# Linear attention beside a top-8 expert layer on one core: order of the first loads, of four VectorE steps in the opening tiles, and of one late scaling

## The chip, the core and the metric

The kernel runs on one core of a Trainium2 chip. A core has five engines that each run their own instruction list in order: TensorE (PE; its weight loads are shown as a lane of their own, PEld), VectorE (DVE), ScalarE (ACT), GpSimd (POOL) and SyncE (SP). An engine waits for another, or for a transfer, only through semaphores; whatever stands behind a waiting instruction on the same engine waits too. Transfers are issued from the lists of SP, ACT and POOL and are carried by 16 DMA engines. The metric is the device time of one execution in microseconds (us), lower is better.

## The reference, cut to what matters

For an input `x` of 2048 tokens by 640 features the result is the sum of `x`, a linear attention of the normalised `x`, and `x` plus the output of an expert layer for its 8 best tokens:

```python
xn = _layernorm(x)                                   # mean, variance, scale per token
q, k, v = split(xn @ wqkv)                           # 32 heads of 20
phi = lambda t: jnp.where(t > 0, t + 1, jnp.exp(t)) + 1e-6
kv  = einsum("bhsd,bhse->bhde", phi(k), v)
z   = einsum("bhsd->bhd", phi(k))
o   = einsum(phi(q), kv) / (einsum(phi(q), z) + 1e-6)
attention = o.reshape(B, S, D) @ wo
r = x @ w_r;  idx = argsort(-r)[:8]                  # 8 tokens for the expert layer
y = (silu(x[idx] @ w_gate) * (x[idx] @ w_up)) @ w_down * sigmoid(r[idx])
return x + attention + (x with y added to its 8 rows)
```

## The kernel before, in words

The order of all work is written out by hand: each engine runs what the program issues to it, in the order of the program. Tokens are cut into 16 tiles of 128 (`t`), features into 5 chunks of 128 (`kc`, `m`).

**Loads.** Lines 109 to 118 issue the first transfers. On SP's list stand half of x tile 0, x tile 1, two chunks of `wk`, x tile 2, `wq` in two pieces by chunk rows (chunks 0 to 2, then 3 and 4; line 117), and x tiles 4 to 7 in one transfer. On ACT's list stand the other half of x tile 0, three chunks of `wk`, and x tile 3 (line 115). The row of the transposes further down (line 198) is issued from SP as well.

**Stage 1, tiles 0 to 15.** For each tile:

- `ln_half` (line 165) takes the statistics of one half of a tile on VectorE; `ln_aggr` (lines 169 to 181) joins them, and GpSimd takes the square root as a power (line 178). For tiles 0 to 3 VectorE does the small steps around it (lines 173, 177, and the reciprocal in line 191); from tile 4 on GpSimd does all four small steps (lines 173, 178, 180, 181).
- `ln_norm` (line 193) writes the normalised tile `xn` on VectorE. Tiles 0 to 2 are transposed on TensorE (line 202) and copied out by ACT or VectorE (line 208). From tile 3 on a DMA transpose from SP writes `xnT` (line 198).
- `k_mm` (line 240) and `q_mm` (line 252) multiply on TensorE. `q_mm` runs over output chunks `m` outside and over `kc` inside, so the first output chunk needs all five row chunks of `wq`, but only columns 0 to 127.
- `phi_act` (lines 215, 218) takes exp and relu on ACT; `phi_vec` (line 227, a SCALAR_TENSOR_TENSOR with two tiles in SBUF as inputs) joins them on VectorE. Its result is `pk` for k, and `pqT` for q.
- `ga_mm` (line 263) multiplies `xn` by `pk` of one tile and sums over tiles in PSUM.

The opening is written out for tiles 0 to 2 (lines 416 to 434). From there the loop of line 437 runs for t = 2 to 15: TensorE gets k of tile t, `ga_mm` of tile t-1, q of tile t; VectorE gets the statistics of tile t+3, the normalisation of tile t+2, `phi_vec` for q of tile t-1, `phi_vec` for k of tile t.

TensorE's list in the opening is: k of tile 0, k of tile 1, q of tile 0, the transposes of tile 2, `ga_mm(0)`, q of tile 1, k of tile 2, `ga_mm(1)`, q of tile 2, k of tile 3, `ga_mm(2)`, and so on.

**Stage 2 and 3.** The sums over all tiles are finished, the 8 tokens are selected, denominators and the expert layer are computed, and `M` is built in five chunks (`m_chunk`, line 743; `m_copy`, line 754). `norm(a, b)` (line 683) scales `pqT` of the output tiles a to b-1 by the reciprocal denominators `rb` on VectorE. It is called for tiles 0 and 1 together ahead of the expert's `py` products (line 766) and of `y_sb` (line 774), and for the others behind `m_copy(3)`. The output products `out_mm` (line 795) then run tile by tile; tile 0 needs the scaled `pqT` of tile 0, tile 1 that of tile 1.

Of the kernel before, what the change touches and what calls it, by code (L numbers as in the profile page):

```python
# [8 lines left out]
P = 128  # L9
S = 2048  # L10
D = 640
# [4 lines left out]
KC = D // P  # L16
# [31 lines left out]
def kernel(  # L48
# [13 lines left out]
    nc = tc.nc  # L62
# [4 lines left out]
    x_v = A_x[0].rearrange("(t p) d -> p t d", p=P)  # L67
    out_v = out[0].rearrange("(t p) d -> p t d", p=P)
    wqkv_v = A_wqkv.rearrange("(kc p) n -> p kc n", p=P)
# [6 lines left out]
    def sb(shape, dt, name, tag=None):  # L76
        return big.tile(shape, dt, tag=tag or name, name=name)
# [4 lines left out]
    def bank(tag, name):  # L82
        return psum.tile([P, TBLK], F32, tag=tag, name=name)

    x_sb = sb([P, T, D], BF16, "x_sb")
# [3 lines left out]
    pk = sb([P, T, D], BF16, "pk")  # L89
    wk = sb([P, KC, D + 1], BF16, "wk")  # L90
    wq = sb([P, KC, D], BF16, "wq")
# [20 lines left out]
    nc.scalar.dma_start(wk[:, 0:3, 0:D], wqkv_v[:, 0:3, D : 2 * D])  # L112
    nc.sync.dma_start(wk[:, 3:KC, 0:D], wqkv_v[:, 3:KC, D : 2 * D])
    nc.sync.dma_start(x_sb[:, 2, :], x_v[:, 2, :])
    nc.scalar.dma_start(x_sb[:, 3, :], x_v[:, 3, :])
    for a, b in ((0, 3), (3, KC)):
        nc.sync.dma_start(wq[:, a:b, :], wqkv_v[:, a:b, 0:D])
    nc.sync.dma_start(x_sb[:, 4:8, :], x_v[:, 4:8, :])


# [41 lines left out]
    def ln_half(t, h):  # L162
        if h == 0:
            stat[t] = work.tile([P, 2, nc.vector.BN_STATS_DIM], F32, tag="stats", name=f"st{t}")
        nc.vector.bn_stats(out=stat[t][:, h, :], in_=x_sb[:, t, h * HW : (h + 1) * HW])  # L165

    def ln_aggr(t):
        mv = work.tile([P, 2], BF16, tag="mv", name=f"mv{t}", bufs=4)
        nc.vector.bn_aggr(out=mv[:], in_=stat[t][:])
        sc = work.tile([P, 2], F32, tag="sc", name=f"sc{t}", bufs=4)  # L170
        sq = work.tile([P, 2], BF16, tag="sq", name=f"sq{t}", bufs=4)
        scal[t] = sc, sq
        (nc.vector if t < LN_FAST else nc.gpsimd).tensor_scalar(  # L173
            out=sq[:, 0:1], in0=mv[:, 1:2], scalar1=EPS_BF16, scalar2=None, op0=ALU.add
        )
        if t < LN_FAST:
            nc.vector.tensor_copy(sc[:, 0:1], mv[:, 0:1])
        nc.gpsimd.tensor_tensor(out=sq[:, 1:2], in0=sq[:, 0:1], in1=half[:], op=ALU.pow)  # L178
        if t >= LN_FAST:
            nc.gpsimd.tensor_tensor(out=sc[:, 1:2], in0=sq[:, 1:2], in1=neg1[:], op=ALU.pow)  # L180
            nc.gpsimd.tensor_copy(sc[:, 0:1], mv[:, 0:1])  # L181

    def ln_stats(t):
        ln_half(t, 0)
        ln_half(t, 1)
        ln_aggr(t)

    def ln_norm(t):
        sc, sq = scal[t]
        if t < LN_FAST:  # L190
            nc.vector.reciprocal(sc[:, 1:2], sq[:, 1:2])
        for a, b in ((0, 2 * P), (2 * P, D)) if t == 0 else ((0, D),):
            nc.vector.tensor_scalar(  # L193
                out=xn[:, t, a:b], in0=x_sb[:, t, a:b], scalar1=sc[:, 0:1], scalar2=sc[:, 1:2],
                op0=ALU.subtract, op1=ALU.mult,
            )
        if t >= PE_TR:
            nc.sync.dma_start_transpose(xnT[:, :, t * P : (t + 1) * P], xn[:, t, :])

    def tr_tile(t, ptr, lo, hi):  # L200
        for kc in range(lo, hi):
            nc.tensor.transpose(
                ptr[:, kc * P : (kc + 1) * P], xn[:, t, kc * P : (kc + 1) * P], ident[:]
            )

    def tr_evict(t, ptr, lo, hi, copy):
        src = ptr[:, 0:D].rearrange("p (k f) -> p k f", k=KC)
        copy(xnT[:, lo:hi, t * P : (t + 1) * P], src[:, lo:hi, :])  # L208
# [3 lines left out]
    def phi_act(ps, tag, between=None):  # L212
        e = work.tile([P, D], BF16, tag="e" + tag, name="e" + tag)
        r = work.tile([P, D], BF16, tag="r" + tag, name="r" + tag)
        nc.scalar.activation(e[:], ps[:, 0:D], AF.Exp)  # L215
        if between is not None:
            between()
        nc.scalar.activation(r[:], ps[:, 0:D], AF.Relu)  # L218
        return e, r

    def phi_vec(dst, er, as3):
        e, r = er
        ea, ra = e[:], r[:]
        if as3:
            ea = ea.rearrange("p (k f) -> p k f", k=KC)
            ra = ra.rearrange("p (k f) -> p k f", k=KC)
        nc.vector.scalar_tensor_tensor(  # L227
            out=dst, in0=ea, scalar=1.0, in1=ra, op0=ALU.min, op1=ALU.add
        )
# [18 lines left out]
    def q_mm(t, tag="B"):  # L248
        ps = pair(tag, f"q{t}")
        for m in range(KC):  # L250
            for kc in range(KC):
                nc.tensor.matmul(  # L252
                    ps[:, m * P : (m + 1) * P],
                    lhsT=wq[:, kc, m * P : (m + 1) * P],
                    rhs=xnT[:, kc, t * P : (t + 1) * P],
                    start=(kc == 0 and m in (0, 4)), stop=(kc == KC - 1),
                    skip_group_check=True,
                )
        return ps

    def ga_mm(t):
        for c in range(3):
            nc.tensor.matmul(  # L263
                gaC[:, c * TBLK : (c + 1) * TBLK] if c < 2 else gaD[:],
                lhsT=xn[:, t, c * P : (c + 1) * P],
                rhs=pk[:, t, 0:TBLK],
                start=(t == 0), stop=(t == T - 1),
            )
# [129 lines left out]
    def k_phi(t, kp, pr=None):  # L398
        ker = phi_act(kp, "k")
        if t < T - 1:  # L400
            nc.scalar.copy(r_all[:, t : t + 1], kp[:, D : D + 1])
        else:
            nc.scalar.copy(rT[:], pr[0:NTB, 0:TBLK])
        return ker
# [10 lines left out]

    kp = k_mm(0, "A", transposes_1)
    ln_aggr(2)
    ln_stats(3)
    ker = k_phi(0, kp)
    kp = k_mm(1, "B")  # L420
    qp = q_mm(0, "A")
    ln_norm(2)
    phi_vec(pk[:, 0, :], ker, False)
    tr2 = bank("D1", "tr2").bitcast(BF16)
    tr_tile(2, tr2, 0, KC)
    ker = k_phi(1, kp)
    eq0 = phi_act(qp, "q", lambda: tr_evict(2, tr2, 0, KC, nc.scalar.copy))
    ln_norm(3)
    ln_stats(4)
    ga_mm(0)  # L430
    phi_vec(pk[:, 1, :], ker, False)
    qp = q_mm(1, "B")
    q_phi(0, eq0)
    qer = phi_act(qp, "q")
# [2 lines left out]
    for t in range(2, T):  # L437
# [22 lines left out]
        ker = k_phi(t, kp, pr)  # L460
# [220 lines left out]
    def norm(a, b):  # L681
        sl = pqT[:, :, a * P : b * P]
        nc.vector.tensor_tensor(out=sl, in0=sl, in1=rb[:, :, a * P : b * P], op=ALU.mult)  # L683
# [52 lines left out]
    def m_chunk(c, tag):  # L736
        pm = Acc(tag, f"M{c}")
        for a, b in halves:
            for g in range(4):
                q = 4 * c + g  # L740
                w = q * GW // KVW
                assert E0[w] <= q * GW // DH * DH and (q * GW + GW - 1) // DH * DH + DH <= E0[w] + P
                nc.tensor.matmul(  # L743
                    pm.at(a, b)[GW * g : GW * g + GW, :],
                    lhsT=kvT[:, q * GW : (q + 1) * GW],
                    rhs=wo[:, w, a:b],
                    start=True, stop=True,
                    tile_position=(0, GW * g),
                )
        return pm  # L750

    def m_copy(c, pm, copy):
        for a, b in pm.spans:
            copy(M[:, c, a:b], pm.at(a, b))
# [2 lines left out]
    m_copy(0, pm0, nc.scalar.copy)  # L757
    pm1 = m_chunk(1, "C")
    m_copy(1, pm1, nc.scalar.copy)
    norm(0, 2)  # L760

    py = pair("A", "py")
    for fc in range(FC):
        j, b = fc // 3, fc % 3
# [20 lines left out]
    m_copy(3, pm3, nc.vector.tensor_copy)  # L785
    pm4 = m_chunk(4, "A")
    m_copy(4, pm4, nc.scalar.copy)
    norm(2, 4)
    norm(4, 8)

# [33 lines left out]
    for t in range(NPRE, T):  # L824
# [6 lines left out]
        else:  # L831
            for i in range(3):
                a, b = LAST[i : i + 2]
# [39 lines left out]
```

## Time and profile before

| | |
|---|---|
| median of 3 runs | 110.91 us (109.94 to 111.06) |
| the profiled execution's own time | 109.81 us |
| its span, from first to last instruction | 108.0 us |
| busy, PE | 102.8 us (95%) |
| busy, PE weight loads | 68.4 us (63%) |
| busy, DVE | 79.9 us (74%) |
| busy, ACT | 66.4 us (61%) |
| busy, POOL | 35.4 us (33%) |
| mean granted TensorE clock | 1.0 |

Rows of the timeline read: start in us from the start of the span, duration in us, engine, line, operation, output and inputs with shapes, number of instructions; a bracket tells how long the engine was idle before it and what ended that. Instructions of an engine overlap a little: the start of the next row can lie before the end of the one ahead. A matmul's recorded duration holds its way through the array, so that the distance between starts tells the rate. Rows of the transfer table give the size and the time from issue to landing. Rows of a table of stretches give for each stretch its length, busy times, granted clock, the share of the 16 DMA engines that was busy, and the rate in GB/s.

### The profile page before, as it was taken

To read this page: it belongs to the slowest core of one execution; us is meant where nothing else is said; L and a number is where in the kernel's file an instruction comes from. 1 tells how busy PE (TensorE), PEld (TensorE's weight loads), DVE (VectorE), ACT (ScalarE), POOL (GpSimd) and SP (SyncE) were. 2 spreads that over 40 slices of the span, in tenths; PEclk is the share of its full clock that TensorE was granted. 3 is DMA by queue.
4 is the path that set the end of the run, shared out by engine and by line. 5 is a ranking of instruction groups with operands and counts; after the bars stand their busy time and mean duration, and the time that the engine had idled before them with its cause. 6 is when DMAs were issued, how large, how long until landed. Compare 5 with 4: busy or idle time off the path is not lost.

```text
span 108.0 us, 2937 instructions
## 1 busy us (share of the span) xinstructions
PE 102.8 (95%) x1132; PEld 68.4 (63%) x1146; DVE 79.9 (74%) x200; ACT 66.4 (61%) x119; POOL 35.4 (33%) x81
## 2 busy tenths in 40 slices
PE   6999999999999999999999999999999999999980
PEld 2547867776677766777677744456996555555550
DVE  3879999979999799987999886814038705938670
ACT  4358977779777797778877855469029455555000
POOL 5423096988897757681000000210003300000000
PEclk9999999999999999999999999999999999999999
DMA  2999053995597999999999991685674798999883
GB/s 67 299 377 345 13 61 61 259 99 155 90 285 154 245 331 204 370 367 187 318 352 394 389 393 53 140 294 116 193 235 150 233 304 262 276 311 393 313 289 122
DMA packets 27406, 25.64 MB, mean 237 GB/s; under 512 B 10880, under 2 KB 25472, under 8 KB 27392
## 3 DMA queue, kind: packets, MB, share of 16 engines
q1 hardware_dynamic: 25232, 23.70, 76.8%
q10 hardware_dynamic: 1984, 1.71, 4.8%
q0 software_dynamic: 176, 0.04, 0.6%
q8 instruction: 9, 0.15, 0.5%
q14 instruction: 5, 0.04, 0.2%
HBM read 17.37 MB, written 5.94 MB: 216 GB/s over the span
## 4 chain that ended last, share of the span: by engine, by line
PE 84%; DVE 9%; DMA 2%; issue 1%; POOL 1%; DVEq 0%
PE q L252 19%; PE k L240 18%; PE o L795 14%; PE gbA L533 6%; PE gaC L263 6%; PE gbC L630 4%; PE gaD L263 3%; DVE st L165 3%; DMA x_sb<-in_A_x_dram 2%; PE gu L643 2%; DVE xn L193 1%; DVE o_all L803 1%; PE pkv L708 1%; PE M L743 1%; PE zp L503 1%
## 5 line engine op out<-in xcount | busy, mean ns | idle before, releaser
L252 PEld LDWEIGHTS <-wq 128*128 128x128 bf16 x400 | 23.6, 98 | 3.6
L240 PE MATMUL k<-wk,xnT 128*128 128x129 bf16 (+1 forms) x152 | 24.5, 296 | 0.5
L252 PE MATMUL q<-xnT,wq 128*128 128x128 bf16 x400 | 25.0, 219 | 0.0
L795 PEld LDWEIGHTS <-pqT 128*128 128x128 bf16 x165 | 12.7, 98 | 9.3 <-issue 0.3
L215 ACT ACTIVATE eq<-q 128x640 bf16<-128x640 f32 x16 | 11.2, 703 | 10.2 <-PE q L252 10.1
L240 PEld LDWEIGHTS <-xnT 128*128 128x128 bf16 x160 | 12.3, 98 | 8.0 <-ACT xnT L208 0.5
L795 PE MATMUL o<-M,pqT 128*128 128x128 bf16 (+1 forms) x108 | 15.7, 298 | 0.1
L165 DVE BATCH_NORM_STATS2 st<-x_sb 128x6 f32<-128x320 bf16 x32 | 14.1, 478 | 1.0 <-DMA x_sb<-in_A_x_dram 1.0
L227 DVE SCALAR_TENSOR_TENSOR pk<-ek,rk 128x640 bf16<-128x640 bf16 x16 | 13.2, 824 | 2.2 <-ACT rk L218 1.7
L178 POOL TENSOR_TENSOR sq<-sq,half 128x1 bf16<-128x1 bf16 x16 | 12.4, 772 | 6.3 <-DVE sq L173 3.2
L227 DVE SCALAR_TENSOR_TENSOR pqT<-eq,rq 128x640 bf16<-128x640 bf16 x16 | 13.1, 818 | 0.2 <-ACT rq L218 0.2
L215 ACT ACTIVATE ek<-k 128x640 bf16<-128x640 f32 x16 | 11.2, 703 | 1.7 <-DVE r_all L441 0.3
L218 ACT ACTIVATE rq<-q 128x640 bf16<-128x640 f32 x16 | 11.2, 700 | 0.0
L218 ACT ACTIVATE rk<-k 128x640 bf16<-128x640 f32 x16 | 11.2, 698 | 0.0
L819 ACT CAST o_all<-o 128x640 bf16<-128x640 f32 x9 | 6.2, 692 | 6.1 <-PE o L795 6.1
L180 POOL TENSOR_TENSOR sc<-sq,neg 128x1 f32<-128x1 bf16 x12 | 9.0, 754 | 0.9
L683 DVE TENSOR_TENSOR pqT<-pqT,rb 128x2560 bf16<-128x2560 bf16 (+1 forms) x5 | 6.0, 1222 | 4.5 <-DMA rb<-rscr 4.4
L263 PE MATMUL gaC<-pk,xn 128*128 128x512 bf16 x31 | 9.3, 377 | 0.1
L581 POOL COPY xsT<-xnT 128x5 bf16 x8 | 1.2, 222 | 20.5 <-DVE zc L583 20.5
L193 DVE TENSOR_SCALAR xn<-x_sb,sc 128x640 bf16<-128x640 bf16 (+2 forms) x17 | 6.9, 410 | 1.0 <-POOL sc L181 0.8
L533 PE MATMUL gbA<-pk,xn 128*128 128x512 bf16 x30 | 7.2, 380 | 0.2 <-issue 0.2
L387 DVE TENSOR_TENSOR x_sb<-x_sb,xn 128x640 bf16<-128x640 bf16 x16 | 7.2, 484 | 0.0
(155 smaller groups left out, 121.7 us busy)
## 6 DMA issues: line engine op xcount, KB each, us to landing
xcp<-x_sb SPq DMA_DIRECT2D x4, 640.0 KB, 7.4
x_sb<-in_A_x_dram SPq DMA_DIRECT2D x3, 640.0 KB, 4.6
x_sb<-xcp SPq DMA_DIRECT2D x3, 640.0 KB, 8.4
out_dram<-o_all SPq DMA_DIRECT2D x11, 160.0 KB, 5.1
wg<-in_B_w_gate_dram SPq DMA_DIRECT2D x2, 768.0 KB, 6.1
wu<-in_B_w_up_dram SPq DMA_DIRECT2D x2, 768.0 KB, 6.8
rb<-rscr SPq DMA_DIRECT2D x5, 256.0 KB, 4.7
rb<-rscr SPq DMA_DIRECT2D x8, 128.0 KB, 3.4
```

Of the source, the lines that this page charges most:

```text
L165: nc.vector.bn_stats(out=stat[t][:, h, :], in_=x_sb[:, t, h * HW : (h + 1) * HW])
L178: nc.gpsimd.tensor_tensor(out=sq[:, 1:2], in0=sq[:, 0:1], in1=half[:], op=ALU.pow)
L180: nc.gpsimd.tensor_tensor(out=sc[:, 1:2], in0=sq[:, 1:2], in1=neg1[:], op=ALU.pow)
L193: nc.vector.tensor_scalar(out=xn[:, t, a:b], in0=x_sb[:, t, a:b], scalar1=sc[:, 0:1], scalar2=sc[:, 1:2], op0=ALU.subtract, op1=ALU.mult,)
L215: nc.scalar.activation(e[:], ps[:, 0:D], AF.Exp)
L218: nc.scalar.activation(r[:], ps[:, 0:D], AF.Relu)
L227: nc.vector.scalar_tensor_tensor(out=dst, in0=ea, scalar=1.0, in1=ra, op0=ALU.min, op1=ALU.add)
L240: nc.tensor.matmul(ps[:, a:b], lhsT=xnT[:, kc, t * P : (t + 1) * P], rhs=wk[:, kc, a:b], start=(kc == 0), stop=(kc == KC - 1),)
L252: nc.tensor.matmul(ps[:, m * P : (m + 1) * P], lhsT=wq[:, kc, m * P : (m + 1) * P], rhs=xnT[:, kc, t * P : (t + 1) * P], start=(kc == 0 an ...
L263: nc.tensor.matmul(gaC[:, c * TBLK : (c + 1) * TBLK] if c < 2 else gaD[:], lhsT=xn[:, t, c * P : (c + 1) * P], rhs=pk[:, t, 0:TBLK], start ...
L533: nc.tensor.matmul(gbA[:, (c - 3) * TBLK : (c - 2) * TBLK], lhsT=xn[:, t, c * P : (c + 1) * P], rhs=pk[:, t, 0:TBLK], start=(t == 0), stop ...
L795: nc.tensor.matmul(ps, lhsT=pqT[:, m, t * P : (t + 1) * P], rhs=M[:, m, a:b], start=(m == M_ORDER[0]), stop=(m == M_ORDER[-1]),)
```

## The change

Four edits:

1. x tile 3 is issued from SP behind x tile 2 and no longer from ACT; `wq` is loaded in two pieces by columns (0 to 383, then 384 to 639, all five row chunks in each) and no longer by row chunks.
2. In the opening, the statistics of tile 3 are split: the first half stays where all of it stood, the second half and the joining step move behind `phi_vec` for k of tile 0.
3. `phi_vec` for k of tile 1 (and `ga_mm(0)` in the program's text) moves ahead of the normalisation of tile 3 and of the statistics of tile 4. No order but VectorE's changes by it: the lists of TensorE, ACT and GpSimd hold the same instructions in the same order.
4. The scaling of the first two output tiles is done one tile at a time: tile 0 where both stood, tile 1 behind `m_copy(4)` in the text, which on VectorE is behind the copy of chunk 3.

VectorE's list in the opening, before: statistics of tile 3 (two halves), joining and its two small steps, reciprocal and normalisation of tile 2, `pk` of tile 0, reciprocal and normalisation of tile 3, statistics of tile 4, joining, `pk` of tile 1, `pqT` of tile 0, statistics of tile 5, joining, normalisation of tile 4, `pqT` of tile 1, `pk` of tile 2.

After: first half of the statistics of tile 3, reciprocal and normalisation of tile 2, `pk` of tile 0, second half, joining and two small steps for tile 3, `pk` of tile 1, reciprocal and normalisation of tile 3, statistics of tile 4, joining, `pqT` of tile 0, and from there as before.

```diff
-    nc.scalar.dma_start(x_sb[:, 3, :], x_v[:, 3, :])
-    for a, b in ((0, 3), (3, KC)):
-        nc.sync.dma_start(wq[:, a:b, :], wqkv_v[:, a:b, 0:D])
+    nc.sync.dma_start(x_sb[:, 3, :], x_v[:, 3, :])
+    for a, b in ((0, 3 * P), (3 * P, D)):
+        nc.sync.dma_start(wq[:, :, a:b], wqkv_v[:, :, a:b])
     nc.sync.dma_start(x_sb[:, 4:8, :], x_v[:, 4:8, :])
...
     kp = k_mm(0, "A", transposes_1)
     ln_aggr(2)
-    ln_stats(3)
+    ln_half(3, 0)
     ker = k_phi(0, kp)
     kp = k_mm(1, "B")
     qp = q_mm(0, "A")
     ln_norm(2)
     phi_vec(pk[:, 0, :], ker, False)
+    ln_half(3, 1)
+    ln_aggr(3)
     tr2 = bank("D1", "tr2").bitcast(BF16)
     tr_tile(2, tr2, 0, KC)
     ker = k_phi(1, kp)
     eq0 = phi_act(qp, "q", lambda: tr_evict(2, tr2, 0, KC, nc.scalar.copy))
+    ga_mm(0)
+    phi_vec(pk[:, 1, :], ker, False)
     ln_norm(3)
     ln_stats(4)
-    ga_mm(0)
-    phi_vec(pk[:, 1, :], ker, False)
     qp = q_mm(1, "B")
...
     m_copy(1, pm1, nc.scalar.copy)
-    norm(0, 2)
+    norm(0, 1)
...
     m_copy(4, pm4, nc.scalar.copy)
+    norm(1, 2)
     norm(2, 4)
     norm(4, 8)
```

## The prediction, made before the changed kernel was run

> **What bounds the kernel now.** I read the page's chain first, because a busy share of 95% for TensorE does not tell whether an opening edit can matter; then the timeline of the opening, engine by engine; then the transfers; last the timeline around the scaling of the output tiles.
>
> ```profile
> span 108.0 us, 2937 instructions
> PE 84%; DVE 9%; DMA 2%; issue 1%; POOL 1%; DVEq 0%
> ```
>
> The chain that ended last lies on TensorE for 84% of the span. TensorE's rows show where it last waited in the opening:
>
> ```profile
> 9.87 1.56 PE L252 MATMUL q<-xnT,wq 128*128 128x128 bf16 x25
> 11.26 0.44 PE L202 MATMUL tr<-ident,xn 128*128 128x128 bf16 x5
> 11.75 0.59 PE L263 MATMUL gaC<-pk,xn 128*128 128x512 bf16 x2
> 12.40 1.56 PE L252 MATMUL q<-xnT,wq 128*128 128x128 bf16 x25
> 17.17 1.26 PEld L240 LDWEIGHTS <-xnT 128*128 128x128 bf16 x10
> 18.61 0.59 PE L263 MATMUL gaC<-pk,xn 128*128 128x512 bf16 x2
> ```
>
> The 25 matmuls of q(0) take 11.26 - 9.87 = 1.39 us, 0.056 each, so the five transposes of tile 2 are through at 11.26 + 0.28 = 11.54. ga(0) starts only at 11.75. That wait of 0.21 us is the last one ahead of the steady loop, and all that the opening edits can win. From there TensorE goes without a gap through q(1), k(2), ga(1), q(2), k(3) (weights at 17.17) and ga(2) at 18.61. Whatever later makes TensorE wait there is lost one for one. The rows that feed it:
>
> ```profile
> 8.91 0.16 DVE L173 TENSOR_SCALAR sq<-mv 128x1 bf16<-128x1 bf16 x1
> 8.98 0.14 DVE L177 CAST sc<-mv 128x1 f32<-128x1 bf16 x1
> 9.15 0.55 POOL L178 TENSOR_TENSOR sq<-sq,half 128x1 bf16<-128x1 bf16 x1 [2.22 <-DVE sq L173]
> 10.33 0.15 DVE L191 RECIPROCAL sc<-sq 128x1 f32<-128x1 bf16 x1
> 10.52 0.45 DVE L193 TENSOR_SCALAR xn<-x_sb,sc 128x640 bf16<-128x640 bf16 x1
> 10.63 0.70 ACT L218 ACTIVATE rk<-k 128x640 bf16<-128x640 f32 x1
> 10.88 0.82 DVE L227 SCALAR_TENSOR_TENSOR pk<-ek,rk 128x640 bf16<-128x640 bf16 x1
> 11.81 0.45 DVE L193 TENSOR_SCALAR xn<-x_sb,sc 128x640 bf16<-128x640 bf16 x1
> 12.17 0.88 DVE L165 BATCH_NORM_STATS2 st<-x_sb 128x6 f32<-128x320 bf16 x2
> 13.08 0.21 DVE L169 BATCH_NORM_AGGREGATE mv<-st 128x2 bf16<-128x12 f32 x1
> 13.21 0.77 DVE L227 SCALAR_TENSOR_TENSOR pk<-ek,rk 128x640 bf16<-128x640 bf16 x1
> 13.48 0.59 POOL L173 TENSOR_SCALAR sq<-mv 128x1 bf16<-128x1 bf16 x1 [2.48 <-DVE mv L169]
> 13.90 0.82 DVE L227 SCALAR_TENSOR_TENSOR pqT<-eq,rq 128x640 bf16<-128x640 bf16 x1
> 14.16 0.98 POOL L178 TENSOR_TENSOR sq<-sq,half 128x1 bf16<-128x1 bf16 x1
> 14.63 0.88 DVE L165 BATCH_NORM_STATS2 st<-x_sb 128x6 f32<-128x320 bf16 x2
> 15.22 0.55 POOL L180 TENSOR_TENSOR sc<-sq,neg 128x1 f32<-128x1 bf16 x1
> 15.73 0.19 POOL L181 CAST sc<-mv 128x1 f32<-128x1 bf16 x1
> 15.95 0.45 DVE L193 TENSOR_SCALAR xn<-x_sb,sc 128x640 bf16<-128x640 bf16 x1 [0.20 <-POOL sc L181]
> 17.05 0.82 DVE L227 SCALAR_TENSOR_TENSOR pk<-ek,rk 128x640 bf16<-128x640 bf16 x1
> ```
>
> pk(0) ends at 10.88 + 0.82 = 11.70, and ga(0) starts 0.05 later: it is what ga(0) waited for. pk(2) ends at 17.87, while ga(2) starts at 18.61: 0.69 us of cover beyond the same 0.05. And xn(4) had to wait for GpSimd's last small step, which ended at 15.92. That chain (VectorE's statistics of tile 4, four small steps on GpSimd, xn(4), then pk(2) behind it on VectorE's list) is the next that can reach TensorE.
>
> One more thing in these rows decides: a GpSimd step of 0.55 us (9.15, beside statistics) takes 0.98 at 14.16, where a SCALAR_TENSOR_TENSOR had begun at 13.90. A clean case later:
>
> ```profile
> 40.70 0.82 DVE L227 SCALAR_TENSOR_TENSOR pk<-ek,rk 128x640 bf16<-128x640 bf16 x1
> 40.71 1.21 POOL L180 TENSOR_TENSOR sc<-sq,neg 128x1 f32<-128x1 bf16 x1
> ```
>
> Begun 0.01 us behind such a step, the same kind of GpSimd step ends at 41.92, 0.40 after VectorE's end at 41.52; the one at 14.16 ends 0.42 after 14.72. So a GpSimd power that starts behind a phi step ends about 0.41 us after it. The short step at 13.48 ends at 14.07, 0.09 after 13.98.
>
> **The change, VectorE's opening.** All times are for the changed kernel, by distances between the rows above.
>
> Tile 2: GpSimd's power still ends at 9.70. VectorE has no second half to do, so the reciprocal starts at 9.73 (not 10.33), xn(2) 0.19 later at 9.92, pk(0) 0.36 later at 10.28, and it ends at 11.10. ga(0) starts at 11.54: gain 0.21.
>
> Tile 3: the second half starts 0.73 after pk(0) started (13.90 to 14.63), at 11.01, and takes half of 0.88 and a little, 0.48; joining at 11.53, small steps at 11.77 and 11.84, then pk(1) at 11.91 (its input from ACT is there at 10.63 + 0.70). GpSimd's power starts 0.24 behind its input step (8.91 to 9.15), at 12.01: 0.10 behind pk(1). It is held until pk(1) ends at 12.73, and ends at 13.14. The reciprocal at 13.17, xn(3) at 13.36, 1.55 later than before, ending at 13.81.
>
> Tile 4: statistics 0.36 later at 13.72, joining at 14.63, pqT(0) 0.13 later at 14.76 to 15.58. GpSimd's first step (0.40 after the joining starts) comes behind pqT(0), and ends at 15.67; power 15.76 to 16.31 beside statistics; inverse 16.39 to 16.94; last step ends at 17.09. xn(4) at 17.12, 1.17 later than before. pk(2) follows 1.10 later (15.95 to 17.05), at 18.22, and ends at 19.04. So ga(2) starts at 19.09 and not at 18.61: **+0.48 us**.
>
> The transposes by DMA, from issue to landing, of tiles 3 and 4:
>
> ```profile
> xnT<-xn SPq DMA_TRANSPOSE x1, 3.4
> xnT<-xn SPq DMA_TRANSPOSE x1, 2.6
> ```
>
> Tile 3 is issued at 13.83 and lands at 17.23. TensorE, 0.21 early, would load k(3)'s weights at 16.96: it waits 0.27. That wait lies inside the other: -0.21 + 0.27 leaves ga(2) ready at 18.67, and it waits 0.42 more for pk(2). Sum: -0.21 + 0.27 + 0.42 = +0.48. Tile 4 is issued at 17.59 and lands at 20.19; k(4) comes one tile of 3.43 us (q 1.39, k 18.61 less 17.17, with the 0.05 from weights to matmul off, 1.39, ga 12.40 - 11.75 = 0.65) after k(3)'s old start, shifted: 21.08. It is covered by 0.9. SP's list holds x tiles 8 to 11 behind that issue; they are late by the same 1.2 us and are wanted three tiles later. Behind ga(2), VectorE has 0.45 + 0.82 + 0.82 + 0.88 + 0.21 = 3.18 us of work per tile of 3.43 us, so its lag shrinks, and the shift of 0.48 gives it more room: no second wait.
>
> The Trainium skill ("SBUF — State Buffer", section "Who interferes with whom") states that a VectorE instruction with two SBUF inputs excludes a GpSimd instruction that reads SBUF, whichever starts first, and gives about 115 ns from VectorE's end until the other proceeds. If the power then ran its whole 0.55, by that page's figure it would end 0.67 after pk(1) and not 0.41, and the short step likewise later, so the sum would be near +1.0 (estimate from the page). The trace's 0.40 and 0.42 decide here.
>
> **The change, loads.**
>
> ```profile
> wq<-in_A_wqkv_dram SPq DMA_DIRECT2D x1, 480.0 KB, 6.2
> wq<-in_A_wqkv_dram SPq DMA_DIRECT2D x1, 320.0 KB, 6.6
> 2.00:2.20 0.20, 1.00 0.88 214
> 8.00:9.00 1.00, 0.99 (x12) 0.57 (x10) 0.96 (x6) 0.91 (x2) 0.00 (x0) 1.00 1.07 364
> ```
>
> `wq` was issued at 2.7 and 3.3, so its pieces landed at 8.9 and 9.9; q(0), behind k(1), began at 9.87 and met both: nothing to win. By columns, 640 runs of 1280 bytes become 640 of 768 and 640 of 512. Price of a run: between 8 and 9 us, 1280 bytes cost 1.07 x 16 us / (364 KB / 1280 B) = 60 ns; between 2.0 and 2.2, when only the 640-byte rows of tile 0 moved, 0.88 x 16 x 0.2 us / (43 KB / 640 B) = 42 ns. Ends: by bytes alone both pieces together cost nothing more; at a fixed 60 ns per run they cost 640 x 60 / 16 = 2.4 us more. I take the line through 42 and 60, nearest in size: 46 and 38 ns, so 640 x 84 / 16 - 640 x 60 / 16 = 0.96 us more, 0.36 of it for the first piece. It lands at 9.3, ahead of 9.87; the second at 10.86, wanted by the sixteenth matmul at 9.87 + 15 x 0.056 = 10.70. A wait of 0.16 in q(0) uses up most of the 0.21, and vanishes in the wait of ga(2). Cost in the sum: 0. x tile 3 goes in the same total of bytes ahead of `wq`; its first half is wanted at about 9.0, and x tile 2 loses a competitor. Cost 0; if tile 3 came late, the first half's step would hold xn(2) by as much, with 0.60 us of cover in pk(0).
>
> The Trainium skill ("DMA: Bandwidth & Descriptors", section "Specifications") puts the size from which a transfer runs at line rate at 512 bytes; by it both pieces would cost nothing more. The 42 ns of 640-byte rows against 60 speak for a part-fixed price; the sum is the same.
>
> **The change, scaling of the output tiles.**
>
> ```profile
> 81.26 0.82 DVE L683 TENSOR_TENSOR pqT<-pqT,rb 128x1280 bf16<-128x1280 bf16 x1
> 82.19 0.32 DVE L774 CAST y_sb<-py 128x160 bf16<-128x160 f32 x1
> 83.48 0.82 DVE L683 TENSOR_TENSOR pqT<-pqT,rb 128x1280 bf16<-128x1280 bf16 x1
> 84.33 0.38 PE L795 MATMUL o1a<-M,pqT 128*128 128x512 bf16 x1
> ```
>
> One tile costs 0.41. Tile 0 is done at 81.67, but y_sb comes no earlier by more than the 0.11 between 82.08 and 82.19, and nothing of its chain bounds. Tile 1's half starts at 83.48 and ends near 83.93; output tile 1 starts at 84.33. Covered by 0.40, cost 0; without that cover at most 0.45.
>
> **Sum.** Against the profiled execution's own 109.81 us (span 108.0): 110.29. The median of the runs shown is 110.91, 1.10 above that execution; with +0.48 it gives 111.4, which I predict.
>
> **Rivals.** (1) Not slower: GpSimd's power gets in ahead of pk(1). It then ends at 12.56, xn(3) comes at 12.85, xn(4) at 16.61, pk(2) ends at 18.53, ga(2) starts at 18.58: -0.03, 109.78. If the first step of tile 4 also escapes pqT(0), pk(2) is in time and the whole gain stays: -0.21, 109.60. The sign turns where pk(2) is late by 0.69 against the old 17.87. For it: the two starts are only 0.10 apart. Against: begun 0.01 behind, 40.71 was held all the same. (2) `wq` late, at the fixed price: second piece at 12.3, q(0) waits 1.6, ga(0) starts at 13.14, +1.39, which swallows the other wait: 111.20 (112.3 from the median). Against it stands the 42 ns. (3) Transposes late: tile 3 costs more only from a landing beyond 3.8 us; tile 4 beyond 3.5; at 3.8 tile 4 gives +0.3 more, 110.6. The x1 rows of 3.4 and 2.6 speak against it. (4) The four edits do nothing: 109.81; VectorE's list is changed as written, so this is small.
>
> **How the numbers follow.** Forecast 0.62, rival 1 0.15, rival 2 0.10, rival 3 0.10, rival 4 0.03. From no change a measurement tells about 1%, 1.1 us. All but rival 2 lie within it; the runs shown scatter by 1.1 us, which takes a tenth of the forecast over the bound. Slower 0.17, same 0.80, faster 0.03 (rival 1 with scatter). Range: lowest run with rival 1, 109.94 - 0.03 = 109.9, to the median with rival 2, 110.91 + 1.39 = 112.3.
>
> **What would show it.** ga(0) straight behind the transposes, pk(0) ending near 11.1; GpSimd's power for tile 3 taking about 1.1 us beside pk(1); xn(3) near 13.4; xn(4) near 17.1, behind GpSimd's last step; ga(2) waiting for pk(2) until 19.1; the steady loop 0.5 late. The forecast is wrong if that power takes 0.55, if a wait for `wq` stands in q(0) beyond 0.7 us, or if k(3) or k(4) waits for its transpose beyond that.

## The result, and the profile after

Over 16 runs each, the changed kernel takes 111.5 us (median, 110.89 to 113.7) and the kernel before 110.22 us (109.58 to 111.8). The ratio is 1.0108 [1.0076, 1.014]: slower by 1.19 us on 110.22. Here and below a ratio leaves out the slow executions that both kernels have now and then, and compares within one series, so it can't be read off the medians beside it, which are over all executions. The forecast was 111.4, built as 0.48 us over no change, so the sign is right and the sum too small. The profiled execution took 111.68 us.

The page of the kernel after, its span and its chain:

```profile
span 110.0 us, 2953 instructions
PE 65%; POOL 14%; DVE 13%; issue 2%; DMA 2%; DVEq 0%; POOLq 0%
```

Against the chain of before (PE 84%, POOL 1%) this says where to look: GpSimd, off the path before, now holds 14% of it, about 15 us. The chain runs on GpSimd almost without a break from 20.12 to VectorE's `xn` of tile 9 at 32.47, which a single wait of half a microsecond in the opening would not explain.

The timeline of the opening, after (start, duration, engine, line, operation; in brackets the idle time ahead and what ended it):

```profile
9.90 1.55 PE L252 MATMUL q<-xnT,wq 128*128 128x128 bf16 x25
10.25 0.82 DVE L227 SCALAR_TENSOR_TENSOR pk<-ek,rk 128x640 bf16<-128x640 bf16 x1
11.57 0.59 PE L263 MATMUL gaC<-pk,xn 128*128 128x512 bf16 x2
11.88 0.81 DVE L227 SCALAR_TENSOR_TENSOR pk<-ek,rk 128x640 bf16<-128x640 bf16 x1
11.99 1.12 POOL L178 TENSOR_TENSOR sq<-sq,half 128x1 bf16<-128x1 bf16 x1 [2.33 <-DVE sc L177]
13.34 0.45 DVE L193 TENSOR_SCALAR xn<-x_sb,sc 128x640 bf16<-128x640 bf16 x1
13.81 1.32 SPq L198 DMA_TRANSPOSE xnT<-xn  x1
16.99 1.26 PEld L240 LDWEIGHTS <-xnT 128*128 128x128 bf16 x10
17.07 0.45 DVE L193 TENSOR_SCALAR xn<-x_sb,sc 128x640 bf16<-128x640 bf16 x1 [0.52 <-POOL sc L181]
18.17 0.82 DVE L227 SCALAR_TENSOR_TENSOR pk<-ek,rk 128x640 bf16<-128x640 bf16 x1
19.04 0.59 PE L263 MATMUL gaC<-pk,xn 128*128 128x512 bf16 x2 [0.45 <-DVE pk L227]
```

ga(0) starts 0.18 earlier than before (11.57 for 11.75), ga(2) 0.43 later (19.04 for 18.61), behind pk(2). TensorE had reached that place 0.18 early, at 18.43, so it lost 0.61 there.

Then the same kernel's timeline of the loop, GpSimd first, then VectorE and TensorE around the second wait:

```profile
20.12 0.30 POOL L173 TENSOR_SCALAR sq<-mv 128x1 bf16<-128x1 bf16 x1 [1.08 <-DVE mv L169]
...
21.58 0.64 POOL L180 TENSOR_TENSOR sc<-sq,neg 128x1 f32<-128x1 bf16 x1
...
22.31 1.63 POOL L327 TENSOR_SCALAR_AFFINE_SELECT cmask<-cmask 128x8 f32<-128x8 f32 x4
...
26.61 0.79 POOL L173 TENSOR_SCALAR sq<-mv 128x1 bf16<-128x1 bf16 x1
27.48 1.20 POOL L178 TENSOR_TENSOR sq<-sq,half 128x1 bf16<-128x1 bf16 x1
...
27.42 0.83 DVE L227 SCALAR_TENSOR_TENSOR pk<-ek,rk 128x640 bf16<-128x640 bf16 x1
...
30.21 0.80 POOL L173 TENSOR_SCALAR sq<-mv 128x1 bf16<-128x1 bf16 x1
...
32.25 0.19 POOL L181 CAST sc<-mv 128x1 f32<-128x1 bf16 x1
...
34.78 0.30 POOL L173 TENSOR_SCALAR sq<-mv 128x1 bf16<-128x1 bf16 x1 [0.58 <-DVE mv L169]
...
32.47 0.45 DVE L193 TENSOR_SCALAR xn<-x_sb,sc 128x640 bf16<-128x640 bf16 x1 [1.53 <-POOL sc L181]
32.83 0.82 DVE L227 SCALAR_TENSOR_TENSOR pk<-ek,rk 128x640 bf16<-128x640 bf16 x1
33.70 0.59 PE L263 MATMUL gaC<-pk,xn 128*128 128x512 bf16 x2 [0.79 <-DVE pk L227]
```

And the rows of the kernel before that answer to these:

```profile
19.00 0.30 POOL L173 TENSOR_SCALAR sq<-mv 128x1 bf16<-128x1 bf16 x1 [1.08 <-DVE mv L169]
...
20.46 0.91 POOL L180 TENSOR_TENSOR sc<-sq,neg 128x1 f32<-128x1 bf16 x1
...
25.52 0.22 POOL L173 TENSOR_SCALAR sq<-mv 128x1 bf16<-128x1 bf16 x1
25.82 0.73 POOL L178 TENSOR_TENSOR sq<-sq,half 128x1 bf16<-128x1 bf16 x1
...
28.55 0.23 POOL L173 TENSOR_SCALAR sq<-mv 128x1 bf16<-128x1 bf16 x1
...
30.13 0.41 POOL L181 CAST sc<-mv 128x1 f32<-128x1 bf16 x1
...
30.58 0.45 DVE L193 TENSOR_SCALAR xn<-x_sb,sc 128x640 bf16<-128x640 bf16 x1
30.94 0.82 DVE L227 SCALAR_TENSOR_TENSOR pk<-ek,rk 128x640 bf16<-128x640 bf16 x1
32.31 0.59 PE L263 MATMUL gaC<-pk,xn 128*128 128x512 bf16 x2
```

GpSimd's power of 27.48 began 0.06 behind a phi step and ended at 28.68, 0.43 after it; before, the same step took 0.73. The bracket at 34.78 is GpSimd's first idle time after 20.12.

The idle time of 1.08 us ahead of 20.12 stands in the kernel before too (19.00). In both, GpSimd waits there for VectorE's statistics of tile 6, and after the change these are 1.12 late as well, so that gap does not work the lag off. A part of it goes where one step is held less: the third step of tile 6 takes 0.64 (21.58) for 0.91 (20.46), and the lag falls from 1.12 to 0.85. From there it grows.

Here is a second wait, which the prediction had excluded. In loop pass 6, VectorE normalises tile 9 ahead of pk(6), and ga(6) needs pk(6). Before, GpSimd's last step for tile 9 ended at 30.54, and pk(6) at 31.76, 0.50 ahead of need (0.55 to the start of ga(6), less the 0.05 from one to the other). After, the same step ends at 32.44, 1.90 later, and pk(6) at 33.65. TensorE came 0.43 later, so 0.93 of it is covered; 0.96 is a wait. From ga(2) to ga(6) TensorE takes 14.66 us for 13.70: the same 0.96.

So TensorE is 1.39 late at ga(6) (-0.18 + 0.61 + 0.96). It stays so: the first output tile starts at 84.34 for 82.96. From the second output tile on it is 1.47. The last rows of TensorE, before and then after:

```profile
103.34 1.53 PE L795 MATMUL o_last<-M,pqT 128*128 128x320 bf16 x15
```

```profile
104.81 1.53 PE L798 MATMUL o_last<-M,pqT 128*128 128x320 bf16 x15
```

From that start to the end of the span it is 4.66 us before and 5.19 after, which makes up the 2.0 between the spans. That tail (VectorE's last step and the last output transfers) lay between 4.4 and 5.8 us in all but one of the experiments' profiles (6.3 there), in no order that the edits explain. So I read TensorE's rows for where time goes, and the ratios for how much.

### The profile page after: what moved, and what is told of

Same layout as the page of the kernel before. It is cut to its first block, busy times and chain, and to the rows that moved or that the text cites. A ratio compares the mean times of both kernels' runs of the same rounds, so it can differ in the third digit from the quotient of the medians.

```text
span 110.0 us, 2953 instructions
## 1 busy us (share of the span) xinstructions
PE 103.3 (94%) x1146; PEld 67.9 (62%) x1146; DVE 79.9 (73%) x201; ACT 66.5 (60%) x119; POOL 35.9 (33%) x81
## 3 DMA queue, kind: packets, MB, share of 16 engines
q10 hardware_dynamic: 1840, 1.55, 4.8%
## 4 chain that ended last, share of the span: by engine, by line
PE 65%; POOL 14%; DVE 13%; issue 2%; DMA 2%; DVEq 0%; POOLq 0%
PE o L798 14%; PE q L252 12%; PE k L240 10%; PE gbA L535 7%; POOL sq L178 6%; PE gaC L263 4%; DVE st L165 4%; PE gbC L632 4%; DVE xn L193 3%; POOL sq L173 2%; POOL sc L180 2%; DMA x_sb<-in_A_x_dram 2%; DVE pk L227 2%; PE gaD L263 2%; PE gu L645 1%
## 5 line engine op out<-in xcount | busy, mean ns | idle before, releaser
L240 PE MATMUL k<-wk,xnT 128*128 128x512 bf16 (+1 forms) x160 | 24.9, 300 | 0.0
L178 POOL TENSOR_TENSOR sq<-sq,half 128x1 bf16<-128x1 bf16 x16 | 13.4, 840 | 7.8 <-DVE sc L177 5.8
L798 PE MATMUL o<-M,pqT 128*128 128x512 bf16 x110 | 15.9, 299 | 0.0
L685 DVE TENSOR_TENSOR pqT<-pqT,rb 128x2560 bf16<-128x2560 bf16 (+2 forms) x6 | 6.1, 1044 | 4.4 <-DMA rb<-rscr 4.4
L180 POOL TENSOR_TENSOR sc<-sq,neg 128x1 f32<-128x1 bf16 x12 | 7.9, 657 | 0.9
L263 PEld LDWEIGHTS <-xn 128*128 128x128 bf16 x48 | 4.1, 96 | 5.2 <-issue 1.6
```

The source lines that it names most:

```text
L240: nc.tensor.matmul(ps[:, a:b], lhsT=xnT[:, kc, t * P : (t + 1) * P], rhs=wk[:, kc, a:b], start=(kc == 0), stop=(kc == KC - 1),)
L263: nc.tensor.matmul(gaC[:, c * TBLK : (c + 1) * TBLK] if c < 2 else gaD[:], lhsT=xn[:, t, c * P : (c + 1) * P], rhs=pk[:, t, 0:TBLK], start ...
L798: nc.tensor.matmul(ps, lhsT=pqT[:, m, t * P : (t + 1) * P], rhs=M[:, m, a:b], start=(m == M_ORDER[0]), stop=(m == M_ORDER[-1]),)
```

## Experiments

**The theory, lag:** tile 3's statistics, put behind pk(0), leave GpSimd about 1 us late. From tile 6 on (20.12) it has no gap until 34.2 (its small steps for the tiles, and in passes 3 to 5 the one-time constants of lines 327 to 342; it has none in the kernel before either, from 19.00 to 32.3), so it cannot catch up; worse, at its new times more of its steps are held by phi steps of VectorE. **The rival, place:** pk(1) ahead of the statistics of tile 4 (edit 3) holds GpSimd's power and delays VectorE's list, and this alone costs what is seen. **A second rival, loads or scaling:** edits 1 and 4 cost part of it. Each run below is compared with the kernel before; "wait" is told from the starts of ga(0), ga(2) and ga(6), whose distances were 6.86 and 13.70 before and 7.47 and 14.66 after. Starts themselves move by up to 0.4 us between executions with the start of the opening.

**Edits 2 and 3 alone.** The changed opening in the kernel before, with its old loads and scaling.

> The kernel before with VectorE's opening order alone (the split statistics of tile 3 and the earlier pk(1)); loads and the scaling of the output tiles as before. Theory G (both waits of TensorE, at ga(2) and at ga(6), come from VectorE's new order through GpSimd's chain): ga(2) at 19.0 to 19.1, ga(6) at 33.6 to 33.8 against 32.31, time +1.2 to +1.5 us, ratio 1.011 to 1.014. Rival L (the loads, by later landings or other transfer traffic, cause the larger second wait): ga(6) at 32.7 to 32.8, +0.4 to +0.5 us.

Ratio 1.0178 [1.0126, 1.0231] (112.15 us; a tail of 5.8 us in its profile), above the forecast of 1.011 to 1.014. Distances 7.46 and 14.65, both waits as in the changed kernel. Its timeline:

```profile
18.99 0.59 PE L263 MATMUL gaC<-pk,xn 128*128 128x512 bf16 x2 [0.45 <-DVE pk L227]
33.64 0.59 PE L263 MATMUL gaC<-pk,xn 128*128 128x512 bf16 x2 [0.69 <-DVE pk L227]
```

Both waits come from the order of VectorE's list. TensorE's last products start at 104.87, as in the changed kernel (104.81), so its rows don't show what the ratio has above 1.0108; the two intervals just overlap, and the excess stays open.

**Edits 1 and 4 alone.** The diff's loads and `norm` lines in the kernel before.

> The kernel before with the other two edits alone: x tile 3 behind tile 2 on SP's list, wq by columns, and the first two output tiles scaled one at a time; VectorE's opening order as before. Theory G: ga(0) still at 11.75, ga(6) at 32.3, output tile 1 at most 0.1 us late, time within 0.2 us of before. Rival L: ga(6) late by 0.7 to 1.0 us, time +0.7 to +1.0. Rival N (the scaling by halves delays the output products): ga(6) unchanged, output tile 1 later by 0.4 against output tile 0.

Ratio 1.0037 [0.9995, 1.0079] (110.64 us). Distances 6.86 and 13.70, and ga(2) and ga(6) stand where they did, at 18.63 and 32.33, without a wait. The loads cost nothing on TensorE, and the interval holds 1. In its profile a transfer of `rb` held the scaling of tiles 4 to 7 for 2.94 us, and TensorE for 0.54. That is not the edit's doing: the profile of edit 2 alone, with the scaling of before, has the same wait with 2.92, and the changed kernel has 1.18.

**The changed kernel with the constants late.** Passes 9 to 11 make the one-time constants, instead of passes 3 to 5:

```diff
-        small_consts(t)
+        small_consts(t - 6 if 9 <= t <= 11 else t if t == 12 else 0)
```

> The changed kernel, with GpSimd's one-time constants (a mask by four selects, two index lists and their casts) moved from the loop passes 3, 4 and 5 to the passes 9, 10 and 11. Theory G (GpSimd has no slack from tile 6 to tile 9 because these constants stand between its small steps, so a lag that enters at tile 4 is not worked off): ga(2) still at 19.0 to 19.1, but no wait at ga(6), which comes at 32.7 to 32.8; time +0.4 to +0.5 us against before. Rival H (GpSimd's lag grows because its steps are held by phi steps of VectorE, whatever else it does): a wait at ga(6) of 0.5 to 1.0 us stays, time +0.9 to +1.4 us.

Ratio 1.008 [1.0045, 1.0115] (111.19 us). Its profile starts late (ga(0) at 11.93 for 11.57), so I read distances: 7.47 and 13.70. The timeline:

```profile
11.93 0.59 PE L263 MATMUL gaC<-pk,xn 128*128 128x512 bf16 x2
19.40 0.59 PE L263 MATMUL gaC<-pk,xn 128*128 128x512 bf16 x2 [0.45 <-DVE pk L227]
33.10 0.59 PE L263 MATMUL gaC<-pk,xn 128*128 128x512 bf16 x2
29.34 0.23 POOL L173 TENSOR_SCALAR sq<-mv 128x1 bf16<-128x1 bf16 x1 [0.69 <-DVE mv L169]
```

The first wait stays, the second is gone, and GpSimd now waits for VectorE (0.69 us at 29.34) where it had worked without a gap. Load on GpSimd in these passes makes the second wait: this is the theory's forecast on the trace. On the clock the gain of 0.96 us doesn't show: 1.008 and 1.0108 have intervals that overlap, and the forecast of +0.4 to +0.5 us was missed, since 0.008 is about 0.9 us. The control that follows costs 0.0043 by itself, about 0.5 us, and the first wait left TensorE 0.43 late; together they would make up the 0.9, but the intervals are too wide to show it.

**The kernel before with the constants late.** The same line, as a control.

> Control: the kernel before with the same constants moved to the passes 9, 10 and 11. Theory G: the order of before leaves 0.5 us of cover at ga(6), so nothing changes on TensorE: ga(6) at 32.3, time within 0.2 us. If the constants in their new place hold up the small steps of later tiles, a wait shows between ga(9) and ga(12) and the time grows by it.

Ratio 1.0043 [1.0012, 1.0073] (110.22 us); TensorE's distances do not change (6.85 and 13.71). The move by itself gains nothing, and its interval lies just above 1, where the forecast was no change. Why it costs 0.4% I have not found: TensorE's rows don't show it.

**Edit 2 alone.** Only the second half and joining of tile 3 behind pk(0); pk(1) where it was.

```diff
-    ln_stats(3)
+    ln_half(3, 0)
...
     phi_vec(pk[:, 0, :], ker, False)
+    ln_half(3, 1)
+    ln_aggr(3)
```

> The kernel before with the split of tile 3's statistics alone: pk(0) earlier, but pk(1) back behind the statistics of tile 4. Theory G (a GpSimd power that starts behind a phi step is held to its end): now no phi step stands behind tile 3's small steps, so its power takes 0.55 us and not 1.12; xn(3) at 12.7 to 12.8 (after: 13.34, before: 11.81), but tile 4's steps are held by pk(1) and pqT(0) as before, so xn(4) near 16.9 (after 17.07, before 15.95); ga(0) at 11.55, ga(2) at 18.8 to 18.9, ga(6) at 33.4 to 33.6, time +1.0 to +1.3 us. Rival P (the place of pk(1) is what costs): ga(2) at 18.4, ga(6) at 32.1, time -0.2 us.

Ratio 1.0106 [1.0059, 1.0154] (111.75 us): as much as the whole change. Its timeline:

```profile
11.92 0.55 POOL L178 TENSOR_TENSOR sq<-sq,half 128x1 bf16<-128x1 bf16 x1 [2.33 <-DVE sc L177]
12.71 0.45 DVE L193 TENSOR_SCALAR xn<-x_sb,sc 128x640 bf16<-128x640 bf16 x1
16.85 0.45 DVE L193 TENSOR_SCALAR xn<-x_sb,sc 128x640 bf16<-128x640 bf16 x1 [0.19 <-POOL sc L181]
18.82 0.59 PE L263 MATMUL gaC<-pk,xn 128*128 128x512 bf16 x2 [0.25 <-DVE pk L227]
33.47 0.59 PE L263 MATMUL gaC<-pk,xn 128*128 128x512 bf16 x2 [0.78 <-DVE pk L227]
```

Without pk(1) in its way, GpSimd's power takes its 0.55 us. Still xn(3) comes at 12.71 for 11.81, xn(4) at 16.85 for 15.95, both 0.90 late, ga(2) waits, and ga(6) is 1.16 late of the 1.39. From ga(2) to ga(6) it is 14.65, the second wait in full. So most of the loss does not need tile 3's power held: it needs tile 3's statistics behind pk(0).

**Edit 3 alone.** pk(1) ahead of the normalisation of tile 3 and the statistics of tile 4; the statistics of tile 3 whole, where they were.

> The kernel before with the earlier pk(1) alone: statistics of tile 3 whole and in their old place, pk(1) ahead of xn(3) and of the statistics of tile 4. Theory G: tile 3's power has begun before a phi step and takes 0.55 us; ga(0) at 11.75 as before; xn(3) at 12.5 to 12.6, xn(4) at 16.2 to 16.4 (0.35 late, since of the two phi steps that held tile 4's GpSimd steps only one is left); ga(2) at 18.61, no wait; ga(6) at 32.3 to 32.9, time 0 to +0.6 us. Rival P (the place of pk(1) is what costs): xn(4) near 17, ga(2) at 19.0, ga(6) at 33.7, time +1.2 us or more.

Ratio 0.999 [0.9939, 1.0041] (110.53 us). Its timeline:

```profile
10.87 1.55 DVE L227 SCALAR_TENSOR_TENSOR pk<-ek,rk 128x640 bf16<-128x640 bf16 x2
16.26 0.45 DVE L193 TENSOR_SCALAR xn<-x_sb,sc 128x640 bf16<-128x640 bf16 x1 [0.51 <-POOL sc L181]
32.30 0.59 PE L263 MATMUL gaC<-pk,xn 128*128 128x512 bf16 x2
```

xn(4) is 0.31 late and no wait follows. The rival (place) falls. A lag of 0.31 was absorbed, one of 0.90 not: GpSimd's third step of tile 6 ended at 21.40, for 21.37 before, because it took 0.63 and not 0.91. The changed kernel loses its 0.27 there in the same way, which was not enough.

**The empty time filled.** In the changed kernel VectorE waits for GpSimd's power 0.21 us ahead of xn(2) and 0.44 ahead of xn(3). Here tile 3's statistics stand whole ahead of xn(2), the joining of tile 3 and tile 4's statistics behind pk(0) while GpSimd works on tile 3, and pk(1) last (against the kernel before):

```diff
-    ln_stats(3)
+    ln_half(3, 0)
+    ln_half(3, 1)
...
     phi_vec(pk[:, 0, :], ker, False)
+    ln_aggr(3)
+    ln_half(4, 0)
+    ln_half(4, 1)
...
     ln_norm(3)
-    ln_stats(4)
+    ln_aggr(4)
     ga_mm(0)
     phi_vec(pk[:, 1, :], ker, False)
```

> The kernel before with another order of VectorE: both halves of tile 3's statistics, xn(2), pk(0), then the joining step and small steps of tile 3, then both halves of tile 4's statistics in the time in which GpSimd takes tile 3's power, then xn(3), the joining step of tile 4, pk(1), pqT(0) and on as before. Theory G: pk(0) ends near 11.3, ga(0) at 11.54; tile 3's power takes 0.55 us beside statistics; the joining step of tile 4 stays near 13.1 and xn(4) near 15.95; no wait at ga(2) (18.40) or ga(6) (32.10): time -0.2 us, ratio 0.998. If x tiles 4 to 7 have not landed by 11.6, the statistics of tile 4 wait and xn(4) is late by the same amount; up to 0.6 us of that is covered at ga(2), less at ga(6).

Ratio 0.9965 [0.9922, 1.0009] (110.01 us). Its timeline:

```profile
11.55 0.55 POOL L178 TENSOR_TENSOR sq<-sq,half 128x1 bf16<-128x1 bf16 x1 [1.89 <-DVE sq L173]
15.66 0.45 DVE L193 TENSOR_SCALAR xn<-x_sb,sc 128x640 bf16<-128x640 bf16 x1 [0.19 <-POOL sc L181]
32.15 0.59 PE L263 MATMUL gaC<-pk,xn 128*128 128x512 bf16 x2
81.45 0.83 DVE L687 TENSOR_TENSOR pqT<-pqT,rb 128x1280 bf16<-128x1280 bf16 x1 [0.40 <-DMA rb<-rscr]
82.20 0.32 DVE L778 CAST y_sb<-py 128x160 bf16<-128x160 f32 x1
```

xn(4) comes 0.29 earlier than before, ga(6) 0.16 earlier, without a wait. The 0.16 is not kept: the scaling of the first two output tiles waits 0.40 for the transfer of `rb`, y_sb stands behind it on VectorE, and output tile 1 starts at 84.33, as before.

**The same with the constants late.**

> The same order of VectorE, with GpSimd's one-time constants moved from the loop passes 3, 4 and 5 to the passes 9, 10 and 11. Theory G: as the run without that move, ga(6) at 32.10, time -0.2 us; if the other order leaves GpSimd late by more than its 0.5 us of cover at ga(6), the run without the move shows a wait there and this one does not.

Ratio 1.0002 [0.9957, 1.0048] (110.35 us). TensorE's distances are 6.85 and 13.71 with the move and without it. Nothing more to win there: without the lag the constants are covered.

**The filled opening with the scaling by single tiles (edit 4).**

> The kernel before with the gap-filled order of VectorE's opening and with the first two output tiles scaled one at a time; loads as before. Theory G with the finding that the two-tile scaling waits for its transfer and then holds y_sb: ga(0) at 11.55 to 11.6, no wait at ga(2) and ga(6); from py to the first output product 1.81 to 1.82 us whatever the transfer does (1.82 to 1.99 in the runs without the split), so TensorE's last products come 0.1 to 0.3 us ahead of before; time -0.1 to -0.4 us, ratio 0.996 to 0.999. Rival: the output stage is bound by transfers, and nothing of it reaches the end: ratio 1.000.

Ratio 0.9991 [0.9959, 1.0023] (110.34 us). The timeline around the scaling:

```profile
82.08 0.33 DVE L778 CAST y_sb<-py 128x160 bf16<-128x160 f32 x1
82.46 0.46 PE L747 MATMUL M<-wo,kvT 128*32 128x512 bf16 x8
83.31 0.69 ACT L758 CAST M<-M 128x640 bf16<-128x640 f32 x1 [0.26 <-PE M L747]
```

y_sb no longer stands behind the scaling (82.08 for 82.20), but ACT now idles 0.26 us ahead of its copy of chunk 4 of M, and output tile 1 starts at 84.32, so the forecast gain on TensorE's last products did not come. That idle time (0.23 to 0.29) stood in every profile with the split, and not in those of before and of the run above, whose copy starts at 83.07. The profile puts it down to TensorE, but TensorE's eight products of chunk 4 are no later: they end at 82.92, for 83.03 in the filled opening without the split. There the copy follows 0.04 behind, here 0.39. What it waits for in that time I have not found.

**The changed kernel with the filled opening**, all else as in the change.

> The changed kernel with the gap-filled order of VectorE's opening in place of its own: its loads, its scaling, none of its two waits. Theory G: ga(0) at 11.6, ga(2) at 18.45, ga(6) at 32.15; time as the run with loads as before, within 0.2 us: the loads cost and win nothing. Rival L (wq by columns, x tiles 4 to 7 landing later): the statistics of tile 4, now wanted at 11.45, wait for their transfer, xn(4) comes late by as much, and a wait shows at ga(2) or ga(6).

Ratio 0.9965 [0.9925, 1.0006] (110.4 us), distances 6.85 and 13.71: no wait of TensorE. The statistics of tile 4 start 0.29 behind the start of tile 3's last small step on VectorE (12.02 and 11.73), where it was 0.06 with the old loads; that is what rival L expects, in small, though no row names the transfer, and it is covered. The ratio is that of the filled opening with the old loads and scaling. With the loads and the scaling of the change still in, the order of VectorE's list takes away the whole loss.

**The changed kernel again**, in the same series.

> The changed kernel once more, beside the two others on the same chip. Theory G: waits at ga(2) near 19.0 and ga(6) near 33.7 again, time +1.1 to +1.5 us against before, ratio 1.010 to 1.014.

Ratio 1.0104 [1.0052, 1.0156] (111.79 us), distances 7.47 and 14.65: both waits are there again.

## Why the prediction was right in sign and wrong in size

- Gain at ga(0): forecast 0.21, measured 0.18 (11.75 to 11.57). Right.
- The opening chain: pk(1) at 11.88 (forecast 11.91), the power 11.99 to 13.11 (12.01 to 13.14), xn(3) at 13.34 (13.36), xn(4) at 17.07 (17.12), pk(2) ending at 18.99 (19.04), ga(2) at 19.04 (19.09). Every step came within 0.05 us, by distances from rows of before. The held power ended 0.42 after pk(1) (forecast 0.41). By the Trainium skill's figure of about 115 ns ("SBUF — State Buffer", section "A bandwidth-pool intuition that's wrong (but worth ruling out)"), added to the whole step, it would have been 0.67 (an estimate from that page of the Trainium skill). That the step is held agrees with the Trainium skill (the same page, section "Who interferes with whom"); its length does not follow from the figure.
- k(3)'s wait of 0.27 for its transpose: it did not come (weights at 16.99). Issued at 13.81, the transpose landed 2.6 us later, at 16.4, where I took the 3.4 of before. The wait was inside the other wait, as the prediction put it, so the sum did not move.
- **The failed step:** "Behind ga(2), VectorE has ... 3.18 us of work per tile of 3.43 us, so its lag shrinks, and the shift of 0.48 gives it more room: no second wait." I counted VectorE's load and left GpSimd's out, though GpSimd was the engine that xn(4) had waited for. VectorE's own lag did shrink as I wrote: pk(2) came 1.12 late, pk(3) 0.86, pk(4) 0.44. GpSimd's did not. Its rows show no gap of its own in the passes that follow, and its lag, 1.12 at xn(4) and 0.85 behind tile 6, grew to 1.90 at tile 9 as steps were held (tile 7's power took 1.03 for 0.57, tile 8's first two steps 0.79 and 1.20 for 0.22 and 0.73, tile 9's first 0.80 for 0.23). The wait of 0.96 at ga(6) is what the sum lacked: 0.43 + 0.96 = 1.39, where 0.48 stood. That the load matters is shown by the run with the constants late (second wait gone); that the lag starts in edit 2 is shown by edit 2 alone.
- The part of pk(1): I took the power held by pk(1) for the deciding point and made its escape rival (1), not slower. Edit 2 alone has the power unheld, and still both waits. pk(1) in its way adds 0.22 at xn(4) (17.07 for 16.85). Whether rival (1) would have met the second wait no run shows: its xn(4) at 16.61 would be 0.66 late, between the 0.31 that was absorbed and the 0.90 that was not.
- Loads: forecast 0 in the sum, and 0 was measured, with a price that was too high. The DMA rows of the kernel after, from issue to landing:

```profile
wq<-in_A_wqkv_dram SPq DMA_DIRECT2D x1, 480.0 KB, 5.8
wq<-in_A_wqkv_dram SPq DMA_DIRECT2D x1, 320.0 KB, 6.5
```

  Issued at 3.2 and 3.7, they landed at 9.0 and 10.2, for forecasts of 9.3 and 10.86, and 8.9 and 9.9 before; half a microsecond of that is the later issue behind x tile 3, which my forecast left out. (By my own 46 and 60 ns the first piece's share of the 0.96 is 0.40 and not 0.36; its landing stays 9.3.) q(0) started at 9.90 and its 25 matmuls went through in the old 1.55. So runs of 768 and 512 bytes moved at nearly the rate of 1280 here. By the rule of the Trainium skill that the prediction set beside its price ("DMA: Bandwidth & Descriptors", section "Specifications"), both pieces cost nothing more; these rows agree with it better than with my price per run. Rival (2) falls.
- Scaling: forecast 0, measured between 0 and 0.1. y_sb comes 0.12 earlier only where `rb` lands late, and chunk 4 of M takes that back.
- The whole: 0.48 was forecast, 1.39 on TensorE and 1.19 [0.84, 1.54] in the runs were measured (the ratio's interval, on 110.22). The predicted 111.4 lies near the measured 111.5 by luck: it started from a median of three runs at 110.91, and the longer series puts the kernel before at 110.22.

## What to carry to other kernels

When an edit makes a chain late, look up the next idle time of every engine in that chain, not only of the one edited: a lag is worked off where an engine has gaps of its own, not where it waits for the late chain itself. A shift also changes which steps are held, and can so let a lag shrink, or grow until a later consumer meets it. Here a wait in the opening was exchanged for a larger one 14 us on. Before moving work behind a critical step, look for the empty time ahead of it: filling that kept the opening's gain without any wait, though nothing measurable was won from it.

## What the runs showed of the hardware

- A GpSimd step of 0.55 us begun behind a SCALAR_TENSOR_TENSOR of VectorE ended 0.40 to 0.43 us after VectorE's end (at 14.16 and 40.71 before, 11.99 and 27.48 after), so a part of its time passes while it is held. Short steps of 0.22 to 0.30 us took 0.79 and 0.80 when they met one.
- Loads with runs of 768 and 512 bytes moved at nearly the rate of 1280-byte runs, though rows of 640 bytes at the start of the kernel had looked dearer per byte (42 ns for half the bytes of 60).
- The time from TensorE's last products to the end of the span varied between 4.4 and 5.8 us in all but one of the profiles of nearly the same code; that is as much as the effects studied here, and the single profile of a kernel should not be used for its total time.
